# The start of an attention and gated-MLP kernel: no block around the program, fewer dummy matmuls from constants, transposes moved, one column block in the accumulators

## The chip, the cores and the metric

The kernel runs on one core of one Trainium2 chip. The metric is the device time of one execution in microseconds (us), over several executions. (A "slow run" below is a run over 1.2 us above the lowest of its own kernel; the others are called quick.) The profile is of one of them, and its times count from the start of the span (the stretch that the trace covers).

Names: PE is the matmul engine and PEld its weight loads, DVE the vector engine, ACT the scalar engine, POOL GpSimd; SP issues most DMAs. PSUM is the memory into which PE writes here: `ps_r` holds a ring of slots in it, `ps_acc` two accumulator banks. SBUF is the memory of the operands. Dummies are matmuls whose result nobody reads; they run before the first data are there, and e6 and e7 show what for.

## The reference, cut to what matters

```python
xn = layernorm(x)                      # x: 2048 x 512, bf16
q  = (xn @ wq)  -> 32 heads x 128      # k_cache, v_cache: 32 heads x 2048 x 128
s  = softmax(q k^T / sqrt(128)) v @ wo
g  = silu( (relu(xn @ W_gate) * (xn @ W_up)) @ W_down )     # F = 1792
out = x + s * g
```

The change touches only the beginning of `g`: the gate and up products of the first 512 rows, while inputs are still arriving, and the frame around the whole program.

## The kernel before: the parts that matter

The first 512 rows are worked in four tiles of 128. Each tile is loaded, centred by DVE (`xc`), transposed by PE, and copied from PSUM to SBUF by ACT (`xcT`). Then PE multiplies it with the first three column blocks of 128 of `W_gate` and `W_up`. The other eleven column blocks are computed 512 rows at a time.

```python
with nc.Block() as block:
    @block.tensor
    def _(_pe_eng):                       # the whole program stands in here
        ...
        warm_w = sem_ln1.sig(dve.memset(warm[:], 0.0))   # operand of the dummies
        load_x0(sp, 0); load_x0(act, 1)
        load_w(sp, Wg_sb, wg_src, sem_wg, 0); load_w(act, Wu_sb, wu_src, sem_wu, 0)
        load_x0(sp, 2); load_x0(act, 3)
        ...
        def head_ln():
            ctok = {0: head_transpose(0, head_center(0))}
            warm_mm(2)
            for n in range(4):
                if n + 1 < 4:
                    ntok = head_center(n + 1)
                _wait(pe, ctok[n])                       # the copy xcT of tile n
                head_tile(n, 0)                          # 4 gate + 4 up matmuls
                if n + 1 < 4:
                    ctok[n + 1] = head_transpose(n + 1, ntok)
                for fc in range(1, HFC):                 # HFC = 3
                    head_tile(n, fc)
        ...
        # column block 3 and later (512 wide) take a slot of a ring of 3 PSUM slots
        s = ring_acquire()                               # slots 0..2 hold blocks 0..2
        gb = 2 * s
        ...
        _wait(pe, warm_w)
        warm_mm(10)                                      # dummy matmuls
        head_ln()
```

The softmax here doesn't subtract the row's maximum and nothing guards it: scores larger than these inputs give would overflow.

## Time and profile before

Three runs before the prediction: median 1286.96 us (1286.47 to 1286.97). The profiled run was another and took 1286.42 us.

| | us | read from |
|---|---|---|
| span of the trace | 1284.6 | page |
| PE busy | 1278.8 | page |
| first dummy, first gate tile, column block 3 start | 1.19, 6.21, 12.83 | timeline of PE |
| PE idle before block 3 | 0.4 | waits |
| SP's last wait, for the closing barrier | 0.2 | waits of SP |

From the page of the kernel before: the span, the busy line (us, share of the span, instructions), and the chain of work that ended last by engine.

```profile
span 1284.6 us, 26946 instructions
PE 1278.8 (100%) x12040; PEld 835.2 (65%) x12040; DVE 380.6 (30%) x685; ACT 1001.7 (78%) x1109; POOL 13.2 (1%) x25
...
PE 99%; DVE 1%; ACT 0%; issue 0%; DVEq 0%
```

PE is the bound. All waits of PE in the whole execution fit into three lines (waiting instruction, what it waited for: us in total, times, longest).

```profile
PE ps_r L374 <- DVE warm L239: 1.2, 1, 1.2
PE ps_r L488 <- ACT gr_sb L454: 0.4, 1, 0.4
PE ps_r L402 <- ACT xcT L369: 0.2, 1, 0.2
```

After column block 3 (L488) has started at 12.83 us, none is listed. So the change can act in two places only: before 12.83 us, and after PE's last work.

The timeline of PE before (start, duration, operation, count, and the idle time before with what ended it). L374 are the dummies, L364 the transposes, L402 the gate and up tiles, L488 column block 3.

```profile
1.19 4.12 PE L374 MATMUL ps_r<-warm 128*128 128x512 bf16 x10 [1.19 <-DVE warm L239]
5.15 0.39 PE L364 MATMUL ps_acc<-ident,xc_sb 128*128 128x128 bf16 x4
5.37 0.59 PE L374 MATMUL ps_r<-warm 128*128 128x512 bf16 x2
6.21 0.40 PE L402 MATMUL ps_r<-xcT,Wg_sb 128*128 128x128 bf16 x4 [0.25 <-ACT xcT L369]
6.45 0.39 PE L402 MATMUL ps_r<-xcT,Wu_sb 128*128 128x128 bf16 x4
6.67 0.39 PE L364 MATMUL ps_acc<-ident,xc_sb 128*128 128x128 bf16 x4
...
12.03 0.39 PE L402 MATMUL ps_r<-xcT,Wu_sb 128*128 128x128 bf16 x4
12.83 1.02 PE L488 MATMUL ps_r<-xcT,Wg_sb 128*128 128x512 bf16 x4 [0.42 <-ACT gr_sb L454]
```

Read the starts, not the durations. A group of four 128-wide matmuls starts every 0.223 us, though each group is shown as 0.39 us long. So the lines overlap by 0.17 us, and the gap in the rhythm of starts before block 3 is 12.83 - 12.03 - 0.223 = 0.58 us, not the 0.42 us listed.

The last waits of SP before:

```profile
SPq L867 <- DMA out_dram<-x_sb: 1.4, 1, 1.4
...
SPq L202 <- PEq L202: 0.2, 1, 0.2
```

The line left out is SP's wait of 0.7 us at the start. L202 is `with nc.Block()`: after the last output has landed, SP waits another 0.2 us at this line for PE's sequencer. This is the closing barrier.

### The profile page before, as it was taken

The page shows a single profiled execution, that of the slowest core. Times are in us where ns is not written, and L with a number is a line of the kernel's source. Part 1 is how long each engine was busy: PE and PEld are TensorE (multiplying, and loading weights), DVE is VectorE, ACT ScalarE, POOL GpSimd, SP SyncE. Part 2 cuts the span into 40 slices and gives each one's busy share as a digit, 9 for nine tenths or more (in the row PEclk, how much of TensorE's full clock was granted, in tenths as well). Part 3 has the DMA queues.
Part 4 walks back from the last instruction along what each step waited for, and adds up shares of the span by engine and source line. Part 5 has one row for each costly group of instructions (what it writes and reads, how often), then busy time and mean ns, then how long its engine had stood idle before and what let it go on. Part 6 is the DMA issues. An engine that isn't in the chain of part 4 may idle for free.

```text
span 1284.6 us, 26946 instructions
## 1 busy us (share of the span) xinstructions
PE 1278.8 (100%) x12040; PEld 835.2 (65%) x12040; DVE 380.6 (30%) x685; ACT 1001.7 (78%) x1109; POOL 13.2 (1%) x25
## 2 busy tenths in 40 slices
PE   9999999999999999999999999999999999999998
PEld 5444476666666666666666666666666666666665
DVE  6433311112222222222222222222222222234455
ACT  3322399998888888888888888888888888888884
POOL 2100000000000000000000000000000000000000
PEclk9999999999999999999999999999999999999999
DMA  9600123232222332332321322323323312333202
GB/s 262 131 1 1 22 48 53 62 55 38 36 53 46 71 55 50 55 70 51 54 47 31 66 47 53 55 67 55 55 51 71 54 34 38 51 67 55 51 13 75
DMA packets 240977, 72.13 MB, mean 56 GB/s; under 512 B 227808, under 2 KB 240864, under 8 KB 240864
## 3 DMA queue, kind: packets, MB, share of 16 engines
q1 hardware_dynamic: 240048, 69.76, 28.5%
q8 instruction: 96, 1.57, 0.5%
q10 hardware_dynamic: 816, 0.66, 0.2%
q14 instruction: 17, 0.14, 0.0%
HBM read 32.77 MB, written 2.10 MB: 27 GB/s over the span
## 4 chain that ended last, share of the span: by engine, by line
PE 99%; DVE 1%; ACT 0%; issue 0%; DVEq 0%
PE ps_acc L742 36%; PE ps_r L645 34%; PE ps_r L578 9%; PE ps_r L599 8%; PE ps_acc L511 4%; PE ps_r L488 4%; PE ps_r L492 4%; PE ps_r L779 1%; DVE fin_tmp L787 0%; PE ps_r L402 0%; PE ps_r L374 0%; DVE x_sb L803 0%; ACT gr_sb L454 0%; PE ps_acc L364 0%; ACT xcT L369 0%
## 5 line engine op out<-in xcount | busy, mean ns | idle before, releaser
L655 ACT ACTIVATE PT<-ps_r 128x1024 bf16<-128x1024 f32 x1024 | 952.5, 1054 | 167.7 <-PE ps_r L645 167.7
L742 PEld LDWEIGHTS ps_acc<-V_sb,PT 128*128 128x128 bf16 x8192 | 620.9, 98 | 241.8 <-ACT PT L655 3.5
L742 PE MATMUL ps_acc<-V_sb,PT 128*128 128x129 bf16 x8192 | 776.9, 220 | 0.0
L645 PE MATMUL ps_r<-QT_sb,KT_sb 128*128 128x512 bf16 x2048 | 754.5, 379 | 0.0
L672 DVE RECIPROCAL rz_sb<-ps_acc 128x4 f32<-128x4 f32 x127 | 23.2, 183 | 729.8 <-PE ps_acc L742 729.8
L645 PEld LDWEIGHTS ps_r<-QT_sb,KT_sb 128*128 128x128 bf16 x2048 | 194.9, 98 | 1.1 <-DVE QT_sb L589 0.4
L578 PE MATMUL ps_r<-xnT,Wq_sb 128*128 128x512 bf16 x512 | 130.9, 379 | 0.0
L599 PE MATMUL ps_r<-Wo_sb,OT_store 128*128 128x512 bf16 x448 | 114.6, 379 | 0.0
L589 DVE CAST QT_sb<-ps_r 128x512 bf16<-128x512 f32 x128 | 88.5, 691 | 48.2 <-PE ps_r L578 48.2
L578 PEld LDWEIGHTS ps_r<-xnT,Wq_sb 128*128 128x128 bf16 x512 | 49.8, 97 | 60.7 <-ACT PT L655 27.1
L675 DVE TENSOR_TENSOR Onorm<-ps_acc,rz_sb 128x512 bf16<-128x512 f32 x127 | 87.8, 691 | 4.4
L599 PEld LDWEIGHTS ps_r<-Wo_sb,OT_store 128*128 128x128 bf16 x448 | 43.8, 98 | 52.9 <-ACT PT L655 0.2
L454 ACT ACTIVATE gr_sb<-ps_r 128x512 bf16<-128x512 f32 x56 | 32.9, 595 | 49.2 <-PE ps_r L488 48.7
L612 DVE TENSOR_TENSOR s_acc<-s_acc,ps_r 128x512 f32<-128x512 f32 x96 | 66.0, 687 | 17.4 <-PE ps_r L599 17.4
L460 DVE TENSOR_TENSOR hT<-gr_sb,ps_r 128x512 bf16<-128x512 bf16 x56 | 38.4, 685 | 46.9 <-PE ps_r L492 42.2
L511 PE MATMUL ps_acc<-Wd_sb,hT 128*128 128x512 bf16 x224 | 49.0, 379 | 0.0
L492 PE MATMUL ps_r<-xnT,Wu_sb 128*128 128x512 bf16 x168 | 43.1, 379 | 0.0
L488 PE MATMUL ps_r<-xnT,Wg_sb 128*128 128x512 bf16 x168 | 43.1, 379 | 0.0
L511 PEld LDWEIGHTS ps_acc<-Wd_sb,hT 128*128 128x128 bf16 x224 | 21.9, 98 | 26.5 <-DVE g_sb L528 0.3
L519 ACT ACTIVATE sig_sb<-ps_acc 128x512 f32<-128x512 f32 x12 | 7.2, 597 | 29.5 <-PE ps_acc L511 29.5
L492 PEld LDWEIGHTS ps_r<-xnT,Wu_sb 128*128 128x128 bf16 x168 | 16.4, 98 | 19.8
L488 PEld LDWEIGHTS ps_r<-xnT,Wg_sb 128*128 128x128 bf16 x168 | 16.4, 98 | 19.8
(50 smaller groups left out, 182.1 us busy)
## 6 DMA issues: line engine op xcount, KB each, us to landing
V_sb<-in_A_v_cache_dram SPq DMA_DIRECT2D x32, 512.0 KB, 4.6
Wq_sb<-in_A_wq_dram SPq DMA_DIRECT2D x32, 128.0 KB, 2.5
Wo_sb<-in_A_wo_dram SPq DMA_DIRECT2D x8, 512.0 KB, 4.9
OT_store<-Onorm SPq DMA_TRANSPOSE x127, 2.4
Wd_sb<-in_B_W_down_dram SPq DMA_DIRECT2D x1, 1792.0 KB, 14.6
x_sb<-in_A_x_dram SPq DMA_DIRECT2D x3, 512.0 KB, 12.1
out_dram<-x_sb SPq DMA_DIRECT2D x6, 256.0 KB, 2.2
Wg_sb<-in_B_W_gate_dram SPq DMA_DIRECT2D x1, 768.0 KB, 12.0
```

Source lines behind the costliest of these rows:

```text
L460: dve.tensor_tensor(hT[par][:, fc, :], gr_sb[gk][:], ps_r[:, gb + 1, :], ALU.mult)
L488: ins = pe.matmul(ps_r[:, gb, :], Wg_sb[:, c, fs], xT[:, c, xs], start=(c == 0), stop=(c == DC - 1))
L492: ins = pe.matmul(ps_r[:, gb + 1, :], Wu_sb[:, c, fs], xT[:, c, xs], start=(c == 0), stop=(c == DC - 1))
L511: ins = pe.matmul(ps_acc[:, jb, 0:D], hT[par][:, fc, j * 128:(j + 1) * 128], Wd_sb[:, fc, :], start=(fc == 0), stop=(fc == FC - 1))
L578: ins = pe.matmul(ps_r[:, bank, :], Wq_sb[b][:, c, :], xnT[:, c, qs], start=(c == 0), stop=(c == DC - 1))
L589: etok = sem_qpe.sig(dve.tensor_copy(QT_sb[b][:, qs], ps_r[:, bank, :]))
L599: ins = pe.matmul(ps_r[:, bank, 0:D], OT_store[g % 2][:, hh, n * 128:(n + 1) * 128], Wo_sb[g % 2][:, hh, :], start=(hh == 0), stop=(hh == ...
L612: dve.tensor_tensor(s_acc[:, n, :], s_acc[:, n, :], ps_r[:, bank, 0:D], ALU.add)
L645: ins = pe.matmul(ps_r[:, 2 * s + tt, :], KT_sb[h % 2][:, t * 128:(t + 1) * 128], QT_sb[h % 2][:, qs], start=True, stop=True)
L655: act.activation(PT[pb][:], ps_r[:, 2 * s:2 * s + 2, :], ACTF.Exp, scale=scale)
L675: dve.tensor_tensor(Onorm[ob][:], o_ap, rz_sb[:].to_broadcast([128, 4, Dh]), ALU.mult))
L742: ins = pe.matmul(o_ap, PT[pb][:, tt, j * 128:(j + 1) * 128], V_sb[vb][:, t, 0:VW], start=(t == 0 and j % 2 == 0), stop=(t == KT - 1 and j ...
```

## The change

The intent was to shorten the front: start the dummies sooner and spend fewer of them, have the next tile's transposes done early, and give column block 3 a place in PSUM for which it need not wait. Only tile 1's transposes move ahead, before the first gate tile. Those of tiles 2 and 3 move back: from after the first column block of the tile before to after its second. The cut also leaves out guards that were taken away and are always true at these sizes.

```diff
-        with nc.Block() as block:
-            @block.tensor
-            def _(_pe_eng):                  # everything moves two levels out
...
-        warm_w = sem_ln1.sig(dve.memset(warm[:], 0.0))
...
-        load_x0(act, 3)
+        load_x0(sp, 3)
...
+        ones_w = nc.const_aps.tensor(1.0, [128, 128], BF16)
+        ones_r = nc.const_aps.tensor(1.0, [128, NQ], BF16)
...
         def head_ln():
-            ctok = {0: head_transpose(0, head_center(0))}
-            warm_mm(2)
+            ctok = [head_transpose(0, head_center(0))]
+            warm_mm(1)
+            ctok.append(head_transpose(1, head_center(1)))
+            ntok = {2: head_center(2), 3: head_center(3)}
             for n in range(4):
-                if n + 1 < 4:
-                    ntok = head_center(n + 1)
                 _wait(pe, ctok[n])
-                head_tile(n, 0)
-                if n + 1 < 4:
-                    ctok[n + 1] = head_transpose(n + 1, ntok)
-                for fc in range(1, HFC):
+                for fc in range(HFC):
                     head_tile(n, fc)
+                    if fc == 1 and n in (1, 2):
+                        ctok.append(head_transpose(n + 1, ntok[n + 1]))
...
-            s = ring_acquire()
+            if Q == 0 and fc == HFC:         # column block 3
+                s = None                     # gate and up go to the two banks of ps_acc
+                _wait_all(pe, acc_free)
+            else:
+                s = ring_acquire()
...
-        _wait(pe, warm_w)
-        warm_mm(10)
+        warm_mm(8)
```

## The prediction

> **What bounds the kernel now.** TensorE. The page gives PE busy for 1278.8 of 1284.6 us, and the chain of waits lies 99% on PE, the clock at full speed. Between 12 and 1265 us the list of waits has one for PE: 0.4 us at 12.4, where column block 3 (the first 512-wide gate matmul) waits until ring slot 0 is evacuated (relu at 11.34, product 12.04 to 12.73; PE resumes at 12.83). From there PE is gapless and unchanged. So the change can act only on the first 12.83 us and on the end.
>
> **What it does** (times from the timeline).
> 1. PE's first dummy waits for the DVE memset of `warm` (0.86 to 1.13) and starts at 1.19. Constants are written before the start barrier, so dummies start near 0.75. This alone saves nothing: real work needs tile 0 centred (4.42+0.35 = 4.77).
> 2. Eight dummies, spaced 0.427, end near 4.15 instead of ten near 5.15. Transposes of tile 0 start near 4.9 instead of 5.15.
> 3. Transposes of tile 1 now precede the first gate tile. They need its centring, which ends at 5.98. So they run 6.05 to 6.28, and gate tiles start at 6.28 instead of 6.21, with one transpose group (0.22) fewer still to do.
> 4. Transposes 2 and 3 come after two of three column blocks of the tile before. From transposes to first use of their copy takes 1.06 us (5.15 to 6.21: 0.42 to the copy, 0.58 copy, 0.06). Before, 1.12 us of PE work covered that. Now 0.67 us does (three groups of 0.223: transposes, one gate, one up). I expect two new PE waits of about 0.4 us, before tiles 2 and 3: +0.8 us.
> 5. Block 3 in the accumulators does not wait for ring slot 0: 0.58 us against an unbroken rhythm goes. Slots are free by block 4.
> Start of block 3: 6.28 + 24 gate/up groups (5.36) + 2 transpose groups (0.45) + two waits (0.78) = 12.87, against 12.83. The front gains about nothing; the waits give back what step 5 brings.
> 6. Without the block, the closing all-engine barrier goes: SP's wait at the block's line is 0.2 us; estimate -0.25 us, serial at the very end.
> 7. The fourth x tile moves from ACT's to SP's queue, delaying later weight loads by about 0.5 us; block 3's land near 10.7, 2 us early. No cost.
>
> **The clock.** [...] dummies are spaced 0.43 up to 4.58 and the next comes after 0.35, so release is near 4.8. Now PE is sparse between 4.15 and 6.05. [...]
>
> **Prediction.** 1286.96 + 0.0 (front) - 0.25 (end) [...] = 1286.8 us, range 1285.4 to 1288.0. Faster by over 2% (26 us) is out of reach: 0.005; within 2% 0.99; slower 0.005.
>
> **What would show it.** First gate tile near 6.28; PE waits on the xcT copy of about 0.4 us before tiles 2 and 3; block 3 near 12.85 with no wait on the relu; four 128-wide matmuls per 0.223 us from 4.9 on; no wait at the block's line at the end.
>
> **What would make it wrong.** A faster copy or earlier tile 1 (up to -0.8 us); late clock release; a costlier block than seen; shifted DMA issues.

The sum came to 1286.96 + 0.0 - 0.25 + 0.1 = 1286.8 us: the term of +0.1 us, for executions in which PE stays slow for longer, was an estimate, and what it rested on is not shown by any run here. The range was given with it in.

"Half rate" and "release of the clock" are names for what the traces show: the 512-wide dummies of the kernel before start every 0.43 us up to 4.58 us, those of column block 3 every 0.216 us (four in 0.86 us, 12.83 to 13.69), and a group of four 128-wide matmuls takes 0.43 or 0.22 us. The granted clock of the profile reads 1.00 both from 0 to 4 us and from 12.5 to 32 us, so that a clock is the cause is not shown. For step 1: POOL writes the bf16 constant from 0.31 to 0.41 us, and the first work of the other engines starts at 0.74 us or later.

## The result, and the profile after

The changed kernel ran five times: 1285.93, 1286.34, 1285.77, 1285.80 and 1287.66 us, median 1285.93. The kernel before, with two more runs beside it, had 1286.37 to 1287.04 and the median 1286.96. The ratio is 0.9997 (95% interval 0.9983 to 1.0011): the same by the 2% rule. Ratios are computed as the mean time of one kernel's runs over that of the other's of the same rounds, so they are not quite the ratio of the medians. That matters here: the median fell by 1.0 us, the mean by only about 0.5 us, because one run is 1.9 us above the lowest. The kernel before spreads too: in all sets together it ran 32 times, 13 times at 1286.28 to 1286.81 us and 19 times at 1286.89 to 1287.18. Its profile is of the lower part; no trace of an upper run was kept, so what sets them apart is open. The two profiled runs differ by only 0.5 us (1286.42 and 1285.93).

The page after (the same lines):

```profile
span 1284.6 us, 26700 instructions
PE 1266.7 (99%) x11810; PEld 834.8 (65%) x12037; DVE 380.3 (30%) x684; ACT 1001.6 (78%) x1109; POOL 13.2 (1%) x25
```

PE busy seems to have fallen by 12 us. It has not: 227 matmul records are missing from this trace (11810 against 12037 weight loads; the page before has 12040 of each), and only three matmuls were taken away. The spans are equal.

The timeline of PE after (L369 dummies, L356 transposes, L396 gate and up tiles, L494 block 3):

```profile
0.77 3.57 PE L369 MATMUL ps_r<-const-bfloat16-1.0 128*128 128x512 bf16 x8 [0.77 <-PEq L886]
4.80 0.38 PE L356 MATMUL ps_acc<-ident,xc_sb 128*128 128x128 bf16 x4 [0.47 <-DVE xc_sb L346]
...
5.92 0.40 PE L356 MATMUL ps_acc<-ident,xc_sb 128*128 128x128 bf16 x4 [0.52 <-DVE xc_sb L346]
6.16 0.39 PE L396 MATMUL ps_r<-xcT,Wg_sb 128*128 128x128 bf16 x4
6.66 0.40 PE L396 MATMUL ps_r<-xcT,Wu_sb 128*128 128x128 bf16 x4
...
8.68 0.39 PE L356 MATMUL ps_acc<-ident,xc_sb 128*128 128x128 bf16 x4
8.91 0.39 PE L396 MATMUL ps_r<-xcT,Wg_sb 128*128 128x128 bf16 x4
9.13 0.39 PE L396 MATMUL ps_r<-xcT,Wu_sb 128*128 128x128 bf16 x4
9.75 0.40 PE L396 MATMUL ps_r<-xcT,Wg_sb 128*128 128x128 bf16 x4 [0.23 <-ACT xcT L361]
...
12.84 0.39 PE L396 MATMUL ps_r<-xcT,Wu_sb 128*128 128x128 bf16 x4
13.28 0.81 PE L494 MATMUL ps_acc<-xcT,Wg_sb 128*128 128x512 bf16 x3
```

Block 3 no longer waits: of its four gate matmuls one record is missing, so it starts at 13.28 - 0.22 = 13.06 us, right behind the last tile. But that is 0.23 us later than before. From the transposes of tile 2 (8.68) PE has two groups of work, then waits until 9.75: 0.40 us beyond the rhythm (9.75 - 9.13 - 0.22). The same stands before tile 3. A further 0.28 us was lost in this execution at 6.66, where the first up weights landed late (5.4 us after their issue, against 5.1 before; PEld waited 0.29 us for them).

The end of SP after:

```profile
SPq L872 <- DMA out_dram<-x_sb: 1.4, 1, 1.4
```

The last DVE instructions, before and then after (start and duration first):

```profile
1281.69 0.75 DVE L803 TENSOR_TENSOR x_sb<-x_sb,fin_tmp 128x512 bf16<-128x512 bf16 x2
```

```profile
1281.92 0.76 DVE L808 TENSOR_TENSOR x_sb<-x_sb,fin_tmp 128x512 bf16<-128x512 bf16 x2
```

The wait for the closing barrier is gone. The last DVE instruction ends at 1282.68 us, 0.24 us later than before (1282.44), and yet the span is the same. From the start of block 3 to that end it takes 1269.6 us in both, so the 0.23 us of the front reach the end undiminished. And a second thing fell: measured time minus span was 1286.42 - 1284.6 = 1.8 us before, and is 1285.93 - 1284.6 = 1.3 us after.

So three questions were open. What is the block worth? Do the new waits cancel the gain of block 3? And what made the run of 1287.66 us?

### The profile page after: what moved, and what is told of

Its sections match the earlier page's. It is cut to its first block, busy times and chain, and to the rows that moved or that the text cites. A ratio compares the mean times of both kernels' runs of the same rounds, so it can differ in the third digit from the quotient of the medians.

```text
span 1284.6 us, 26700 instructions
## 1 busy us (share of the span) xinstructions
PE 1266.7 (99%) x11810; PEld 834.8 (65%) x12037; DVE 380.3 (30%) x684; ACT 1001.6 (78%) x1109; POOL 13.2 (1%) x25
## 4 chain that ended last, share of the span: by engine, by line
PE 85%; ACT 12%; issue 1%; DVE 1%; DMA 0%; ACTq 0%; DVEq 0%
PE ps_acc L747 32%; PE ps_r L650 25%; ACT PT L660 12%; PE ps_r L583 9%; PE ps_r L604 8%; PE ps_acc L517 4%; PE ps_r L498 3%; PE ps_r L494 3%; PE ps_r L784 1%; DMA Wu_sb<-in_B_W_up_dram 0%; DVE fin_tmp L792 0%; PE ps_r L396 0%; DVE x_sb L808 0%; ACT xcT L361 0%; PE ps_acc L498 0%
## 5 line engine op out<-in xcount | busy, mean ns | idle before, releaser
L650 PE MATMUL ps_r<-QT_sb,KT_sb 128*128 128x512 bf16 x1837 | 675.1, 379 | 0.3
L494 PE MATMUL ps_r<-xnT,Wg_sb 128*128 128x512 bf16 x165 | 42.6, 379 | 0.2
L494 PEld LDWEIGHTS ps_r<-xnT,Wg_sb 128*128 128x128 bf16 x168 | 16.4, 98 | 19.8
```

The source lines that it names most:

```text
L494: ins = pe.matmul(g_ps, Wg_sb[:, c, fs], xT[:, c, xs], start=(c == 0), stop=(c == DC - 1))
L650: ins = pe.matmul(ps_r[:, 2 * s + tt, :], KT_sb[h % 2][:, t * 128:(t + 1) * 128], QT_sb[h % 2][:, qs], start=True, stop=True)
```

## The experiments

Ten kernels ran, each with five timed runs, and each set beside runs of the kernel before, whose medians were 1286.89 to 1286.96 in every set. All gave correct results.

### e1: only the block taken away

```diff
-        with nc.Block() as block:
-            @block.tensor
-            def _(_pe_eng):
```

> The kernel before with only the block taken away (nothing else). Theory A (the block costs [...] a closing barrier that lies partly in the profile's span and partly after it): about 0.7 us faster, of which about 0.25 us in the span and about 0.45 us between span and measured time (that difference was 1.82 us before and 1.33 us after). Rival B (only the 0.2 us barrier in the span): 0.25 us faster and the difference between time and span stays at 1.8. The front is unmoved in both: block 3 starts at 12.8 us.

Measured: median 1286.18 (1285.45 to 1286.62), against 1286.89: 0.7 us less. Time minus span was 1.28 to 1.35 us in all five runs. From the end of DVE's last instruction to the end of the span it took 1.95 us, against 2.16 before. In this profile block 3 starts at 13.32 us (13.54 less one matmul), not 12.8: the first weights landed late (gate 5.0 us after its issue and up 5.7, against 4.4 and 5.1 before; PE waited 0.6 us for gate and 0.2 us for up). That part of the expectation missed. Late up weights also stand in the profiles of the changed kernel and e3, but not in those of the five other kernels without a block, so the landing varies between executions; that the block has no part in it is not shown. Theory A holds for the end of the program.

### e4: the changed kernel with the block put back

```diff
+        with nc.Block() as block:
+            @block.tensor
+            def _(_pe_eng):
```

> The changed kernel with the block put back around it. Theory A: about 0.7 us slower than the changed kernel, 0.25 in the span and the difference between time and span back at 1.8 us; the front unmoved [...]. Rival B: only 0.25 us slower. A rival on the dummies: the block's start costs PE more than 0.2 us.

Measured: median 1286.64 (1286.39 to 1288.16), 0.7 us above the changed kernel. Time minus span is back at 1.76 to 1.86 us, and the closing wait is back in the span:

```profile
SPq L877 <- DMA out_dram<-x_sb: 1.4, 1, 1.4
SPq L201 <- PEq L201: 0.2, 1, 0.2
```

Over all kernels that ran after the prediction, the difference between time and span is 1.27 to 1.36 us in the 40 runs without a block and 1.75 to 1.87 us in the 15 runs with one, with nothing in between. From the last DVE instruction to the end of the span it takes 1.88 to 1.98 us in the eight profiles without a block and 2.16 to 2.22 us in the four with one. So the block costs about 0.25 us in the span and 0.5 us behind it. At the start it costs nothing visible: the first dummy starts at 0.77 us here as in the changed kernel.

### e2: only column block 3 in the accumulators

```diff
+        if Q == 0 and fc == HFC:
+            s = None
+            _wait_all(pe, acc_free)
+        else:
+            s = ring_acquire()
```

> The kernel before with only column block 3 put in the accumulators. Theory: PE's idle of 0.4 us before block 3 goes, it starts at about 12.25 us instead of 12.83, and the whole run is 0.58 us faster, as PE is gapless from there on. Rival: the gain is eaten by a later wait (block 4 or the down products waiting for the accumulators): block 3 early, but the first down product at the old 31.8 us.

Measured: median 1286.30 (1286.01 to 1286.39), 0.6 us below the kernel before. The profile has no wait before block 3, and PE has no other new wait. From the first gate tile (6.64) to block 3 (12.90 less one matmul = 12.68) it took 6.04 us, against 12.83 - 6.21 = 6.62 before: the 0.58 us of the gap. The absolute start was not 12.25, since the first transposes ran late (5.43 us, against 5.15 before) and partly at half rate in this execution (0.37 us for the group). So intervals from the first gate tile are the better measure, and they are used below. The rival falls: the first down product came at 31.67 us against 31.82 before, earlier by the 0.15 us by which block 3 is earlier here (12.68 against 12.83). At the end of the execution the last two DVE instructions are earlier by the same (1281.54 against 1281.69).

### e3 and e5: the transposes of tiles 2 and 3 earlier or later

```diff
-                    if fc == 1 and n in (1, 2):
+                    if fc == 0 and n in (1, 2):      # e3; in e5: fc == 2
```

After the first column block is where the kernel before had these transposes, so e3 takes back this part of the change.

> The changed kernel with the transposes of tiles 2 and 3 put after the first instead of the second column block. Theory: the two PE waits of 0.4 us on the xcT copy go (cover 1.12 us against 1.06 needed), block 3 starts 0.8 us sooner, about 12.3 us, and the run is 0.8 us faster than the changed kernel, about 1285.2. Rival: tile 2 is centred too late (x tile 2 landed at 6.8), PE waits on the centring instead, and nothing is gained.

> The changed kernel with the transposes of tiles 2 and 3 put after the last (third) column block of the tile before, so that nothing but the 0.22 us of the transposes themselves covers the 1.06 us to the copy's use. Theory: each of the two PE waits grows from 0.4 to 0.84 us, block 3 starts 0.9 us later than in the changed kernel, and the early-release runs stand at about 1286.7 (changed kernel 1285.8, the early one 1285.2). Rival: the waits are set by the x tiles' landing, and then it is no slower than the changed kernel.

Measured, e3: median 1285.43 (1285.10 to 1287.04); its three quick runs are at 1285.10, 1285.22 and 1285.43, 0.5 to 0.7 us below the quick runs of the changed kernel, where 0.8 was expected (e8 below shows where the rest is). e5: three runs at 1286.72 to 1286.74, and two slow ones at 1288.41 and 1288.48. Median with median, e5 is 0.8 us above the changed kernel (1286.74 against 1285.93). In e5 the waits are visible at full size:

```profile
9.05 0.39 PE L356 MATMUL ps_acc<-ident,xc_sb 128*128 128x128 bf16 x4
10.11 0.40 PE L396 MATMUL ps_r<-xcT,Wg_sb 128*128 128x128 bf16 x4 [0.68 <-ACT xcT L361]
```

PE waits 0.84 us beyond the rhythm (10.11 - 9.05 - 0.22), as expected. From transposes to first use is 1.06 us here, 1.07 us in the changed kernel (8.68 to 9.75), and at e3's position the wait on the copy is not listed at all. The chain of transposes, copy and use takes 1.06 us; what counts is how much PE work stands inside it: 0.22, 0.67 or 1.12 us. The rival (arrival of the x tiles) falls.

The profiled run of e3 happened to be one of its two slow ones, 1287.04 us, and it shows what a slow run is. The timeline of PE:

```profile
0.77 3.57 PE L369 MATMUL ps_r<-const-bfloat16-1.0 128*128 128x512 bf16 x8 [0.77 <-PEq L886]
...
7.62 0.63 PE L396 MATMUL ps_r<-xcT,Wg_sb 128*128 128x128 bf16 x4
8.05 0.63 PE L396 MATMUL ps_r<-xcT,Wu_sb 128*128 128x128 bf16 x4
...
9.75 0.57 PE L396 MATMUL ps_r<-xcT,Wu_sb 128*128 128x128 bf16 x4
10.16 0.39 PE L356 MATMUL ps_acc<-ident,xc_sb 128*128 128x128 bf16 x4
10.38 0.39 PE L396 MATMUL ps_r<-xcT,Wg_sb 128*128 128x128 bf16 x4
```

Until 10.1 us a group of four takes 0.43 us, after that 0.22 us: PE ran at half rate in the first 10 us. The granted clock of the profile reads 1.00 from 0 to 4, 4 to 8 and 8 to 12 us all the same; the spacing of matmuls is the witness.

### e6 and e7: no dummies, and the old number of dummies

```diff
-        warm_mm(8)       # e6: removed; e7: warm_mm(10)
...
-            warm_mm(1)   # e6: removed; e7: warm_mm(2)
```

> The changed kernel with no dummy matmul at all. Theory (clock): the four slow runs of fifteen of the eight-dummy kernels (1287.66, 1287.04, 1286.65, 1288.16) are executions in which the clock was released only near 10 us, as the profile of e3 shows. Without dummies every execution is released late, so all runs are 1.3 to 2.5 us above 1285.8: 1287.1 to 1288.3, and the profile shows 128-wide groups of 0.43 us until 8 to 11 us. Rival (data arrival): the slow runs come from late landing of x and weights; then this kernel runs as the changed one, four of five below 1286.4.

> The changed kernel with the old number of dummies, ten and two instead of eight and one, still from constants. PE is then busy from 0.77 to about 5.7 us but for short gaps. Theory (clock): no slow run: all five within 0.8 us of the lowest, median 1285.9 (the dummies fit in idle PE time, as tile 1's centring ends only at 5.9). Rival (data arrival): one or two of five at 1287 or more, as with eight.

Measured, e6: 1287.06 to 1288.13, median 1287.62; every run is 1.3 to 2.4 us above the lowest of the changed kernel (1285.77), so all stand at the slow level, though none is over 1.2 us above its own lowest. Its profile shows half rate (0.43 us a group) until about 8.6 us:

```profile
7.83 0.63 PE L395 MATMUL ps_r<-xcT,Wu_sb 128*128 128x128 bf16 x4
8.26 0.55 PE L395 MATMUL ps_r<-xcT,Wg_sb 128*128 128x128 bf16 x4
8.65 0.39 PE L395 MATMUL ps_r<-xcT,Wu_sb 128*128 128x128 bf16 x4
```

e7: 1285.83, 1286.11, 1285.81, 1285.79 and 1285.82. No slow run, and the quick level is that of the changed kernel (1285.77). Ten and two dummies cost nothing over eight and one, because PE waits for the centring of tiles 0 and 1 anyway (0.15 and 0.30 us):

```profile
0.77 4.06 PE L369 MATMUL ps_r<-const-bfloat16-1.0 128*128 128x512 bf16 x10 [0.77 <-PEq L886]
4.99 0.38 PE L356 MATMUL ps_acc<-ident,xc_sb 128*128 128x128 bf16 x4 [0.15 <-DVE xc_sb L346]
5.21 0.60 PE L369 MATMUL ps_r<-const-bfloat16-1.0 128*128 128x512 bf16 x2
6.11 0.40 PE L356 MATMUL ps_acc<-ident,xc_sb 128*128 128x128 bf16 x4 [0.30 <-DVE xc_sb L346]
```

Counting as slow a run over 1.2 us above its own kernel's lowest, the four kernels with eight and one dummies (changed, e3, e4, e5) have 6 slow runs of 20, each 1.5 to 1.9 us above. The two with ten and two dummies from constants (e7 and e8, below) have none of 10. By itself that could be chance (if 6 runs of 30 are slow, none falls among a given 10 in 7% of cases), but the other kernels with ten and two dummies have none either: none of 20 in e1, e2, e9 and e10, none of 32 in the kernel before. In e1 and e9 the runs spread over 1.2 and 1.1 us, so the line at 1.2 us is a choice. Only one slow run of the six was profiled, e3's; that the other five were late in the same way is inferred from their size and from e6 and e7.

### e9 and e10: the gains alone, and the constants alone

e9 is the kernel before with e1's and e2's edits together. e10 is the kernel before with its ten and two dummies taken from constants:

```diff
-        _wait(pe, warm_w)
-        pe.matmul(ps_r[:, 2 * NSLOT - 1, 0:D], warm[:, 0:128], warm[:], start=True, stop=True)
+        pe.matmul(ps_r[:, 2 * NSLOT - 1, :], ones_w, ones_r, start=True, stop=True)
```

> The kernel before with the block taken away and block 3 in the accumulators, and nothing else: its own order of transposes, its own ten and two dummies behind the memset. Theory: these two parts are what the change gains, and they add: 0.7 from the block and 0.55 from the accumulators give a median of 1285.6, below the changed kernel's mean of 1286.3 and without slow runs above 1286.3. Rival: the gains overlap, or the rest of the change (constants, fewer dummies, transposes ahead) gains too; then this stands near 1286.0.

> The kernel before with its ten and two dummies taken from the constants, so that PE starts at about 0.77 instead of 1.19 us; nothing else. Theory: the first real transposes wait for the centred tile (4.7 to 4.8 us), and the first gate tiles for the weights (landing at 5.6 to 6.6), so an earlier start of the dummies is worth at most 0.25 us: median 1286.6 to 1286.9. Rival: the earlier release of the clock is worth as much as the earlier start, 0.4 us or more: below 1286.5.

Measured, e9: median 1285.69 (1285.27 to 1286.38), mean 1285.87. The two parts add: 1.24 us against 0.71 + 0.59 for e1 and e2 in the medians, 0.93 against 0.60 + 0.47 in the means. Two runs stood at 1286.36 and 1286.38, just above the 1286.3 of the expectation. Without the rest of the change the mean is 0.4 us below that of the changed kernel (1286.30). e10: median 1286.54 (1286.35 to 1286.70), 0.4 us below the 1286.93 of its set. The expectation was 1286.6 to 1286.9, and the rival's was below 1286.5: it lies between them. In the means the gain is 0.25 us (1286.55 against 1286.80), and the runs of the two kernels overlap, so it is a hint. In its profile, which is of the slowest of its five runs, the first gate tile started at 6.30 us, no sooner than in the kernel before (6.21), and its first group took 0.39 us (0.24 before), so the gain is not visible there. Whether a sooner clock or a better average of arrival times made it stays open.

### e8: what the runs pointed to

The changed kernel with e3's and e7's edits.

> The changed kernel with transposes after the first column block and with ten and two dummies: what the runs so far point to. Theory: 0.8 us from the waits and no late clock: median 1285.2, all five runs below 1286.0, mean 1.4 us below the kernel before. Rival: the clock is also late here in some runs, mean near e3's 1285.9.

Measured: 1285.26, 1285.25, 1285.14, 1285.53 and 1285.54; median 1285.26 against 1286.96 before, ratio 0.9988 (0.9976 to 1.0001). It is the best kernel, 1.7 us below the kernel before in the median. By ratio it is still the same within 2%, and the interval just includes 1. From the first gate tile to block 3 it takes 5.81 us against e7's 6.61, so the two waits were worth the full 0.80 us. In the medians e8 is 0.56 us below e7; in its profile the first gate tile starts 0.25 us later (6.59 against 6.34), because half rate lasts to about 6.5 us (the transposes of tile 0 take 0.43 us, those of tile 1 0.32, the first gate group 0.23). So ten and two dummies did not end half rate at once in this execution; it was over when the gate tiles began. The waits of PE in its whole execution are one line, the time before the dummies:

```profile
PE ps_r L369 <- PEq L886: 0.8, 1, 0.8
```

### All of them in one table

| kernel | dummies | block | median us | mean us | runs over 1.2 us above own lowest | first gate tile to block 3, us |
|---|---|---|---|---|---|---|
| before | 10+2 | yes | 1286.96 | 1286.76 | 0 of 5 | 6.62 |
| changed | 8+1 | no | 1285.93 | 1286.30 | 1 of 5 | 6.90 (0.28 of it waiting for weights) |
| e1 | 10+2 | no | 1286.18 | 1286.11 | 0 of 5 | 6.96 (0.35 of it waiting for weights) |
| e2 | 10+2 | yes | 1286.30 | 1286.25 | 0 of 5 | 6.04 |
| e3, transposes earlier | 8+1 | no | 1285.43 | 1285.89 | 2 of 5 | 7.88 (half rate to 10.1) |
| e4 | 8+1 | yes | 1286.64 | 1286.86 | 1 of 5 | 6.61 |
| e5, transposes later | 8+1 | no | 1286.74 | 1287.42 | 2 of 5 | 7.50 |
| e6 | none | no | 1287.62 | 1287.62 | 0 of 5, all at the slow level | 7.60 (half rate to 8.6) |
| e7 | 10+2 | no | 1285.82 | 1285.87 | 0 of 5 | 6.61 |
| e8, transposes earlier | 10+2 | no | 1285.26 | 1285.34 | 0 of 5 | 5.81 |
| e9 | 10+2 | no | 1285.69 | 1285.87 | 0 of 5 | 6.06 |
| e10 | 10+2 | yes | 1286.54 | 1286.55 | 0 of 5 | 6.77 (first group near half rate) |

The last column is from each one's timeline: the start of block 3 (the first listed start, less 0.216 us where its first record is missing) minus that of the first gate tile.

## Why the prediction was right or wrong

The measured median of 1285.93 us lies in the range of 1285.4 to 1288.0, and "within 2%" was right. The range was wide, though (2.6 us), for a forecast change of -0.15 us; measured were -1.03 us in the median and -0.46 in the mean. Step by step:

- **What bounds it, and where the change can act: right.** No wait of PE changed after block 3.
- **Steps 1 and 2: the times right, "this alone saves nothing" not confirmed.** Dummies from 0.77 us, transposes of tile 0 at 4.80 (predicted near 4.9). But e10, which changes the dummies' operand alone, was 0.4 us lower in the median and 0.25 in the mean; with the spread of the kernel before this is a hint and not shown.
- **Step 3: right.** First gate tile at 6.16 (predicted 6.28), because in this execution the first x tile landed 0.11 us sooner (DVE begins on it at 3.36 us, against 3.47 before).
- **Step 4: right, and the largest term of the front.** Two waits of 0.40 us each were predicted, and 0.40 us each was measured (9.75 - 9.13 - 0.22, and the same before tile 3). e5, the changed kernel and e3 confirm the 1.06 us chain by covering it with 0.22, 0.67 and 1.12 us of work, and e8 against e7 gives the 0.80 us (6.61 - 5.81).
- **Step 5: right.** 0.58 us; e2 measured it alone as 6.62 - 6.04.
- **The front's sum: right.** From first gate tile to block 3 the prediction had 12.87 - 6.28 = 6.59 us; e4 and e7 show 6.61, and the changed kernel 6.90 with 0.28 us of waiting for weights. So the gain of block 3 was given back by the two waits.
- **Step 6: the mechanism right, the size wrong.** The term was -0.25 us and measured about -0.75. The 0.25 us in the span was right. The other 0.5 us lies between the end of the span and the measured time, where no line of the profile shows it. The prediction took the span for the whole of the time.
- **Step 7: no cost was shown, but it was not tested alone.** The late up weights of this profile also occur without it (e1), occur with it (e3) and are absent with it (e4 to e8).
- **The clock: the term too small.** The sum had +0.1 us for it, the author's estimate; measured are +1.5 to +1.9 us in 6 of 20 executions, about +0.5 on average. In e3's profile half rate lasted until 10.1 us.

The two errors of size nearly cancel in the mean (-0.5 and +0.4 us), which is luck, and not in the median, which passes over the slow runs. The mean of 1286.30 is still 0.5 us below the predicted 1286.8. Of this 0.2 us is the base: the prediction started from a median of three, 1286.96, where the mean of the kernel before is 1286.76. The rest is of the size of e10's hint; that it is the same thing is not shown.

## What to carry to other kernels

When a kernel is at its bound nearly everywhere, list the few waits of the bounding engine and ask of each part of a change which of them it ends and which new one it makes; here one gap of 0.58 us went and two of 0.40 us came. A PE transpose that goes through a copy takes about 1.1 us from its start to the copy's first use here, so put it that much PE work ahead. Part of a change can be worth taking back: with the transposes of tiles 2 and 3 at their old place and the old number of dummies, the median fell by another 0.7 us (e8). Don't economise on warm-up matmuls where PE would idle anyway (here ten and two ran at the same quick level as eight and one, 1285.79 against 1285.77 us, and had no slow run in 10 against 6 in 20), and look at the spread of runs, not at the best one, when you change their number.
